# Cross attention and Fourier mixing on one core: the first batch's tables, layer 1 and stores put in another order

## The chip, the cores and the metric

The kernel runs on one core of a Trainium2 chip. TensorE (PE, with its weight loads PEld), VectorE (DVE), ScalarE (ACT), GpSimd (POOL) and SyncE (SP) each work through their own list of instructions in order and wait for each other on semaphores. The metric is the time on the device in microseconds (us), lower is better.

## The reference

Two blocks follow each other. The first is attention in both directions between 512 positions and 32 states, in 8 batches of 8 heads with 64 columns:

```python
scores = scale * np.matmul(x, state.transpose(0, 1, 3, 2))
a = softmax(scores);   xread = np.matmul(a, state)
scores2 = scale * np.matmul(state, x.transpose(0, 1, 3, 2))
a2 = softmax(scores2); sread = np.matmul(a2, x)
return np.concatenate([xread, sread], axis=2)        # 8 x 8 x 544 x 64
```

The second takes the 544 rows of 512 columns of each batch through a two-dimensional Fourier transform, a normalisation and two layers:

```python
mixed = np.real(np.fft.fft(np.fft.fft(x, axis=1), axis=2))
u = x + mixed
un = (u - mu) / np.sqrt(var + 1e-06)
return u + np.maximum(un @ w_ch1, 0.0) @ w_ch2        # 512 -> 2048 -> 512
```

## The kernel before

Each batch goes through three parts. `attend(b)` turns the states and x on PE (`turn_state`, `turn_x`: tiles sTp and xTp, copied to sT and xT), forms the exponentials twice (ET by state, E by position), reads with them (`xread`, `sread`: tiles xrp, xfp, xlp, srp, which become the rows XR, XF, XL) and folds the rows (XE, XO, XN). `transform(b)` multiplies the folded rows with cosine and sine tables over the 544 rows (`over_s`, tiles gp, copied to G) and then with tables over the 512 columns (`over_d`, T2, tiles yp), adds the rows (U), takes mean and variance, centres (ub) and turns the result (tiles tp, copied to unT). A batch has four tiles of 128 rows: row block k in 0 and 1, as it stands or mirrored (r = 1); the 32 rows left over in the middle, the low rows, are gathered over four batches. `layer1` and `layer2` are the two layers (tiles ph, which ACT brings to hT, and po, which VectorE scales by the row's deviation and adds to U in `store`).

The tables are made on the chip before the first batch needs them: a counter times a row number is brought into one period ("turned") on VectorE, `turn` for the 544 rows and `second_turn` for the 512 columns; ACT takes sines of both (`sines`, `more_sines`), and two of the four column tables are quarter turns of the other two, eight strided multiplications on POOL.

The order of every engine is written out by hand: `weave` takes streams of steps, each with a begin and an end between 0 and 1, and issues all steps by their place. `warm(n)` adds n matmuls on the identity matrix whose result nobody reads; `warmed` puts them behind each step of a stream. Loads of x go out on SP's queue (for batch 0 partly on ACT's); one small load puts row 0 into a partition that a large load has just filled, so it waits for that load. The weights are loaded by POOL, behind small copies into `gate` that hold POOL back. A mirrored tile is first written to `r_dram` and copied from there to the output in reversed row order; the low rows go through `l_dram` in the same way. In the last batch the mirrored tiles are stored on ACT's queue. Buffers for ot are 4, psum tiles with tag c 3, with tag q 3, and one pair of banks for x.

Of the kernel before, what the change touches and what calls it, by code (L numbers as in the profile page):

```python
# [12 lines left out]
F32 = mybir.dt.float32  # L13
BF16 = mybir.dt.bfloat16
I32 = mybir.dt.int32
AF = mybir.ActivationFunctionType
# [12 lines left out]
def kernel(  # L29
# [67 lines left out]
    def load_x(b):  # L97
        xs = wk.tile([128, 4, dm], F32, name="xs", tag="xs")
        xb = x[b].rearrange("h s d -> s h d")
        for n, (ps, si, rows) in enumerate((  # L100
            (slice(0, 128), 2, xb[256:384]),
            (slice(0, 128), 0, xb[1:129]),
            (slice(0, 1), 2, xb[0:1]),
            (slice(0, 128), 1, xb[129:257]),
            (slice(0, 128), 3, xb[384:512]),
        )):
            queue = nc.scalar if b == 0 and n in (1, 4) else nc.sync
            queue.dma_start(out=xs[ps, si, :].rearrange("p (h d) -> p h d", d=D), in_=rows)
        xs_of[b] = xs

    def cast_x(b):
        xs, t = xs_of[b], xin_bufs[b % 2]
        if b == 0:
            for si in (0, 2, 1, 3):
# [84 lines left out]

    def second_turn():  # L200
        nc.vector.tensor_copy(l2, li)
# [21 lines left out]
    def more_sines():  # L223
        w = 2.0 * PI / dm * shrink
        nc.scalar.activation(T2[:, 0, :], q2_, AF.Sin, bias=halfpi, scale=-w)
        nc.scalar.activation(T2[:, 2, :], f2, AF.Sin, bias=0.0, scale=-w)
        nc.scalar.activation(gate2[:, 3:4], gate2[:, 0:1], AF.Exp)
        c4 = [T2[:, i, :].rearrange("p (n r) -> p r n", r=4) for i in range(4)]
        for r in range(4):
            near, far = (0, 2) if r % 2 == 0 else (2, 0)  # L230
            for o, i, sign in ((1, near, 1.0 if r < 2 else -1.0), (3, far, 1.0 if r in (0, 3) else -1.0)):
                nc.gpsimd.tensor_scalar(c4[o][:, r, :], in0=c4[i][:, r, :], scalar1=sign, scalar2=None, op0=ALU.mult)
# [37 lines left out]
    def more_states():  # L270
        nc.vector.memset(stb[:, 2:].rearrange("p b g c -> p (b g c)").bitcast(F32), 0.0)
        state_ones(2, B)

# [17 lines left out]
    def attend(b):  # L291
# [19 lines left out]
        def turn_x(g):  # L311
            p = qt("xTp", BF16)
            for si in (0, 2, 1, 3):
                for k in range(2):
# [107 lines left out]
    def transform(b):  # L422
# [72 lines left out]
        if b == 0:  # L495
# [3 lines left out]
                lambda: (add(0, 0), centre(0, 0), turn_u(0, 1)),  # L499
                lambda: turn_u(0, 0),  # L500
                lambda: (add(1, 1), centre(1, 1)),
                lambda: (add(1, 0), centre(1, 0), turn_u(1, 1)),
                lambda: (turn_u(1, 0), done())]
# [45 lines left out]
    def layer1(key):  # L549
# [15 lines left out]

        def half_step(i, r):
            ph = psF.tile([128, 512], F32, name="ph", tag="c")
            cols = slice(256 * r, 256 * r + 256)
            for f in (2 * i, 2 * i + 1):
                for c in range(DC):  # L570
                    nc.tensor.matmul(ph[:, 256 * (f % 2):256 * (f % 2) + 256], lhsT=w1[:, c, f * 128:(f + 1) * 128],  # L571
                                     rhs=un_of[key][:, c, cols], start=(c == 0), stop=(c == DC - 1))
            nc.scalar.activation(hT[:, 2 * i:2 * i + 2, cols], ph.rearrange("p (a b) -> p a b", b=256), AF.Relu,
                                 scale=-1.0 if key in flipped else 1.0)

        if key == 0:
            return [lambda i=i, r=r: half_step(i, r) for r in range(2) for i in range(FC // 2)]
        return [lambda i=i: step(i) for i in range(FC // per)]

    def layer2(key):  # L580
# [4 lines left out]
        def store(i, cols):  # L585
# [7 lines left out]
            elif isinstance(dst, int):  # L593
                nc.sync.dma_start(out=l_dram[dst].rearrange("b r n -> (b r) n"), in_=ot)
                rows = out[4 * dst:4 * dst + 4]
                nc.sync.dma_start(out=rows[:, 257:288, :].rearrange("b r n -> r b n"),
                                  in_=l_dram[dst][:, 1:NL, :].rearrange("b r n -> r b n"))
                nc.sync.dma_start(out=rows[:, 0:1, :], in_=l_dram[dst][:, 0:1, :])
            else:
# [3 lines left out]
                queue.dma_start(  # L603
                    out=out[b, top:top - 128:-1, :].rearrange("r (c n) -> c r n", c=8),
                    in_=r_dram[b, k].rearrange("r (c n) -> c r n", c=8))

# [37 lines left out]
    def warmed(steps, n):  # L644
        return [lambda s=s: (s(), warm(n)) for s in steps if s is not None]
# [10 lines left out]
    weave((warmed(t0[4:8], 2), 0, 1), (s1[3:4], 0, 0))  # L656
# [53 lines left out]
```

## Time and profile before

| | us |
|---|---|
| median of 3 runs | 364.56 (364.07 to 364.62) |
| the profiled execution's own time | 364.14 |
| its span in the profile | 362.4 |
| PE busy | 325.5 (90%) |
| DVE busy | 175.8 (49%) |
| ACT busy | 158.6 (44%) |
| POOL busy | 65.6 (18%) |

A row of the timeline gives start, duration, engine, line, operation, output<-input, shapes, count, and in brackets the idle time before it with what ended it. Engine names with a q (SPq, ACTq) are queues that issue transfers: the duration there is that of the issue, not of the transfer. Matmul rows that follow each other overlap by about 0.2 us, since a result leaves the array after the next has begun. A row by stretch gives its length, the busy time of each engine with the number of instructions, the granted clock of TensorE as a share of full speed, the mean busy share of the 16 DMA engines and GB/s.

### The profile page before, as it was taken

What the parts mean: (1) busy time and instruction counts of PE and PEld (TensorE: products, weight loads), DVE (VectorE), ACT (ScalarE), POOL (GpSimd) and SP (SyncE); (2) the same over time, 40 slices, a digit from 0 to 9 for tenths busy, and PEclk for the clock granted to TensorE, in tenths of its full rate; (3) what the DMA queues carried; (4) which work ended last, traced back from release to release, by engine and by line L of the source; (5) the groups of instructions that cost most, each with busy time, mean ns of one, the idle gap of its engine ahead of it and who ended that gap; (6) DMA issues with size and microseconds to landing.
All of it is one profiled execution on the core that took longest, in us unless ns stands there. A gap on an engine that the chain in (4) does not pass through costs nothing.

```text
span 362.4 us, 5627 instructions
## 1 busy us (share of the span) xinstructions
PE 325.5 (90%) x2198; PEld 189.8 (52%) x2232; DVE 175.8 (49%) x432; ACT 158.6 (44%) x299; POOL 65.6 (18%) x150
## 2 busy tenths in 40 slices
PE   6747688899999999998999999999999999979970
PEld 6725566655555555555555555545554544445450
DVE  7697465645475537661454628462847173000120
ACT  4852664943464346333464345534553342433100
POOL 4099820500050003200140004000300030000000
PEclk9967899999999999999999999999999999999996
DMA  6889997005211511043101122020202020211123
GB/s 126 166 131 167 182 193 145 2 29 131 60 45 56 127 52 56 31 123 113 29 31 37 52 58 60 29 59 29 58 31 59 31 58 37 81 38 51 61 78 93
DMA packets 61556, 27.11 MB, mean 75 GB/s; under 512 B 52698, under 2 KB 57050, under 8 KB 61530
## 3 DMA queue, kind: packets, MB, share of 16 engines
q1 hardware_dynamic: 52874, 20.99, 22.4%
q0 software_dynamic: 4224, 4.19, 7.1%
q10 hardware_dynamic: 4432, 1.57, 1.8%
q8 instruction: 17, 0.28, 0.3%
q14 instruction: 9, 0.07, 0.1%
HBM read 22.04 MB, written 13.63 MB: 98 GB/s over the span
## 4 chain that ended last, share of the span: by engine, by line
PE 78%; DVE 11%; ACT 4%; DMA 2%; issue 2%; SPq 0%; DVEq 0%; ACTq 0%
PE po L622 30%; PE ph L561 27%; PE gp L439 3%; PE yp L457 3%; PE ph L571 2%; DMA xs<-in_x_dram 2%; PE xTp L316 2%; PE eTp L325 2%; PE srp L372 2%; PE tp L481 2%; DVE st L282 1%; ACT ub L474 1%; PE po L614 1%; PE xfp L353 1%; PE xrp L353 1%
## 5 line engine op out<-in xcount | busy, mean ns | idle before, releaser
L622 PE MATMUL po<-w,hT 128*128 128x512 bf16 x482 | 122.6, 379 | 1.6 <-ACT hT L563 0.9
L563 ACT ACTIVATE hT<-ph 128x512 bf16<-128x512 f32 x112 | 66.8, 597 | 121.2 <-PE ph L561 117.2
L561 PE MATMUL ph<-unT,w 128*128 128x512 bf16 x434 | 113.7, 379 | 2.9 <-ACT hTL L563 1.4
L561 PEld LDWEIGHTS <-w 128*128 128x128 bf16 x576 | 51.3, 98 | 55.6 <-issue 4.8
L622 PEld LDWEIGHTS <-hT 128*128 128x128 bf16 x496 | 47.7, 98 | 45.1 <-issue 1.3
L588 DVE SCALAR_TENSOR_TENSOR ot<-po,rstd,U 128x512 f32<-128x512 f32 (+1 forms) x33 | 24.2, 733 | 46.4 <-PE po L622 41.3
L449 POOL COPY GL<-G 128x128 bf16<-128x128 bf16 x8 | 2.4, 300 | 151.6 <-ACT G L447 151.6
L463 DVE TENSOR_TENSOR U<-yp,XR 128x511 f32<-128x511 f32 x16 | 10.9, 683 | 25.7 <-PE yp L457 24.6
L282 DVE BATCH_NORM_STATS2 st<-U 128x6 f32<-128x512 f32 x32 | 21.8, 680 | 0.1
L287 POOL TENSOR_TENSOR rstd<-rstd,mhalf 128x1 f32<-128x1 f32 x34 | 20.1, 591 | 2.7
L447 ACT CAST G<-gp 128x288 bf16<-128x288 f32 x30 | 11.9, 398 | 19.1 <-PE gp L439 13.1
L286 POOL TENSOR_TENSOR rstd<-mv,epst 128x1 f32<-128x1 f32 x34 | 6.6, 193 | 67.8 <-DVE mv L284 67.8
L483 ACT COPY unT<-tp 128x512 bf16<-128x512 bf16 x32 | 18.4, 588 | 0.4 <-PE tp L481 0.2
L317 DVE COPY xT<-xTp 128x1024 bf16<-128x1024 bf16 x10 | 6.9, 691 | 22.6 <-PE xTp L316 22.5
L571 PE MATMUL ph<-unT,w 128*128 128x256 bf16 x128 | 17.3, 282 | 0.5 <-ACT unT L483 0.5
L642 PE MATMUL warm<-ident 128*128 128x128 bf16 x144 | 14.2, 249 | 3.7 <-POOL halfpi L80 3.4
L457 PE MATMUL yp<-T,G 128*128 128x512 bf16 x60 | 16.1, 379 | 0.2
L481 PE MATMUL tp<-ident,ub 128*128 128x128 bf16 x128 | 11.8, 219 | 4.7 <-ACT ub L474 3.8
L383 ACT ACTIVATE XR<-srp,rcs 32x64 bf16<-32x64 f32 x32 | 9.9, 310 | 12.6 <-DVE rcs L374 12.3
L642 PEld LDWEIGHTS <-ident 128*128 128x128 bf16 x144 | 11.8, 114 | 6.3 <-POOL halfpi L80 3.4
L481 PEld LDWEIGHTS <-ub 128*128 128x128 bf16 x128 | 9.0, 98 | 10.3 <-ACT ub L474 4.5
L571 PEld LDWEIGHTS <-w 128*128 128x128 bf16 x128 | 12.6, 101 | 2.5 <-issue 0.7
(139 smaller groups left out, 391.0 us busy)
## 6 DMA issues: line engine op xcount, KB each, us to landing
xs<-in_x_dram SPq DMA_DIRECT2D x30, 256.0 KB
w<-in_moe_w_ch_dram POOLq DMA_DIRECT2D x8, 512.0 KB, 9.1
out_dram<-ot SPq DMA_DIRECT2D x15, 256.0 KB
r_dram<-ot SPq DMA_DIRECT2D x14, 256.0 KB
out_dram<-r_dram SPq DMA_DIRECT2D x14, 256.0 KB
xs<-in_x_dram ACTq DMA_DIRECT2D x2, 256.0 KB
l_dram<-ot SPq DMA_DIRECT2D x2, 256.0 KB
r_dram<-ot ACTq DMA_DIRECT2D x2, 256.0 KB
```

The lines of the kernel that those rows point to most:

```text
L282: nc.vector.bn_stats(st6, u)
L287: nc.gpsimd.tensor_tensor(rstd, rstd, mhalf, op=ALU.pow)
L447: nc.scalar.copy(G[:, j, :], p[:, 0:NM])
L457: nc.tensor.matmul(yp, lhsT=G[:, c, 128 * k:128 * k + 128], rhs=T2[:, c, :], start=(c == 0), stop=(c == 3))
L481: nc.tensor.transpose(tp[:, 128 * j:128 * j + 128], ub[k, r][:, 128 * j:128 * j + 128], ident)
L483: nc.scalar.copy(unT[:, :, col:col + 128], tp[:, 0:512].rearrange("p (a b) -> p a b", b=128))
L561: nc.tensor.matmul(ph[:, o:o + n], lhsT=w1[:, c, f * 128:(f + 1) * 128], rhs=un_of[key][:, c, :], start=(c == 0), stop=(c == DC - 1))
L563: nc.scalar.activation(hT[:, per * i:per * i + per, :].rearrange("p a b -> p (a b)"), ph, AF.Relu, scale=-1.0 if key in flipped else 1.0)
L571: nc.tensor.matmul(ph[:, 256 * (f % 2):256 * (f % 2) + 256], lhsT=w1[:, c, f * 128:(f + 1) * 128], rhs=un_of[key][:, c, cols], start=(c == ...
L588: nc.vector.scalar_tensor_tensor(ot[:, cols], in0=po_of[i][:, 0:cols.stop - cols.start], scalar=rstd, in1=u[:, cols], op0=ALU.mult, op1=AL ...
L622: nc.tensor.matmul(po_of[i], lhsT=h_of[key][:, f, i * 128:(i + 1) * 128], rhs=w2[:, f, :], start=(f == 0), stop=(f == FC - 1))
L642: nc.tensor.matmul(t[:, 0:128], lhsT=ident, rhs=ident, start=(i == 0), stop=(i == n - 1))
```

## The change

Eight edits, the first six in the front, up to the end of batch 0:

- The one-row load of x goes last of the five in each batch, no longer between the large ones; the casts and turns of x follow that order.
- The second turn runs right behind the first one, ahead of sT's and xT's copies. POOL's first gate waits for its end.
- Of the eight quarter turns four go to ACT.
- `warmed` bursts behind the last three score steps go; 48 warming matmuls come at the end of batch 0's reads. POOL's cast of batch 1's x moves ahead of the low rows' tables.
- The clearing of the state blocks of batches 2 to 7 moves from VectorE to POOL, the ones in it (eight small memsets on VectorE) into layer 1's stretch.
- Layer 1 of batch 0 goes tile by tile: 16 steps of four 128-column products for one tile of rows, instead of 16 steps of two 256-column products for two tiles.
- The places of the streams beside layer 1 of batch 0 shift, and layer 1 of batch 1 begins at 0.08 of its stage instead of 0.02.
- Mirrored tiles are copied in 16 column pieces of 32 (before: 8 of 64), low rows in 16 column pieces by batch (before: whole rows, outermost the row number).

VectorE's order at the start. gen is the scratch of the two turns (128x864 the first, 128x512 the second); before:

```order
L175 SCALAR_TENSOR_TENSOR gen_78<-gen_78 128x864
L309 COPY sT<-sTp 128x512
L317 COPY xT<-xTp 128x1024 x2
L201 CAST gen_79<-gen_79 128x512
L202 TENSOR_SCALAR gen_79<-gen_79,pf 128x512
L203 TENSOR_SCALAR gen_79<-gen_79 128x512
L204 TENSOR_SCALAR gen_79<-gen_79 128x512
L205 TENSOR_TENSOR gen_79<-gen_79 128x512
L175 SCALAR_TENSOR_TENSOR gen_79<-gen_79 128x512
L133 CAST stb<-stf 32x2x64 x4
L361 RECIPROCAL rs<-xrp 128x8
```

And now, on the same engine at the same place:

```order
L175 SCALAR_TENSOR_TENSOR gen_78<-gen_78 128x864
L201 CAST gen_79<-gen_79 128x512
L202 TENSOR_SCALAR gen_79<-gen_79,pf 128x512
L203 TENSOR_SCALAR gen_79<-gen_79 128x512
L204 TENSOR_SCALAR gen_79<-gen_79 128x512
L205 TENSOR_TENSOR gen_79<-gen_79 128x512
L175 SCALAR_TENSOR_TENSOR gen_79<-gen_79 128x512
L308 COPY sT<-sTp 128x512
L316 COPY xT<-xTp 128x1024 x2
L133 CAST stb<-stf 32x2x64 x4
L360 RECIPROCAL rs<-xrp 128x8
```

The six rows of the second turn moved from between xT and the first reciprocal to ahead of sT.

ACT's order where layer 1 of batch 0 begins (ub is the centred tile, unT its turned copy, hT layer 1's result, ET and E belong to batch 1); before:

```order
L474 ACTIVATE ub<-U,mv 128x512 x2
L483 COPY unT<-tp 128x4x128 x2
L573 ACTIVATE hT<-ph 128x2x256
L327 ACTIVATE ET<-eTp 128x512
L474 ACTIVATE ub<-U,mv 128x512 x2
L483 COPY unT<-tp 128x4x128
L573 ACTIVATE hT<-ph 128x2x256
L341 ACTIVATE E<-esp 128x512
```

Now:

```order
L473 ACTIVATE ub<-U,mv 128x512 x2
L482 COPY unT<-tp 128x4x128
L572 ACTIVATE hT<-ph 128x4x128
L482 COPY unT<-tp 128x4x128
L572 ACTIVATE hT<-ph 128x4x128
L473 ACTIVATE ub<-U,mv 128x512
L326 ACTIVATE ET<-eTp 128x512
L572 ACTIVATE hT<-ph 128x4x128
```

The first result of layer 1 now comes behind one copy of unT, and two more come before batch 1's second ET and the third ub.

SP's order at the end of the program, from the last batch's low rows on; before:

```order
L594 DMA l_dram<-ot 128x512
L596 DMA out_dram<-l_dram 31x4x512
L598 DMA out_dram<-l_dram 4x512
L592 DMA out_dram<-ot 128x512
L592 DMA out_dram<-ot 128x256 x2
```

Now:

```order
L593 DMA l_dram<-ot 128x512
L595 DMA out_dram<-l_dram 16x31x32 x4
L597 DMA out_dram<-l_dram 16x4x32
L591 DMA out_dram<-ot 128x512
L591 DMA out_dram<-ot 128x256 x2
```

One copy of 31 rows by four batches became four copies with 16 as the outermost count. On ACT's queue the two mirrored tiles of the last batch change from 8x128x64 to 16x128x32 at unchanged places.

The diff, cut:

```diff
-            (slice(0, 1), 2, xb[0:1]),
             (slice(0, 128), 1, xb[129:257]),
             (slice(0, 128), 3, xb[384:512]),
+            (slice(0, 1), 2, xb[0:1]),
...
-    def second_turn():
+    def turn2():
...
-        state_blocks(1, 2, nc.vector.tensor_copy)
+
+    turn2()
...
-            for o, i, sign in ((1, near, 1.0 if r < 2 else -1.0), (3, far, 1.0 if r in (0, 3) else -1.0)):
-                nc.gpsimd.tensor_scalar(c4[o][:, r, :], in0=c4[i][:, r, :], scalar1=sign, scalar2=None, op0=ALU.mult)
+            nc.scalar.activation(c4[1][:, r, :], c4[near][:, r, :], AF.Copy, scale=1.0 if r < 2 else -1.0)
+            nc.gpsimd.tensor_scalar(c4[3][:, r, :], in0=c4[far][:, r, :], scalar1=1.0 if r in (0, 3) else -1.0,
+                                    scalar2=None, op0=ALU.mult)
...
-    nc.gpsimd.tensor_copy(gate, q1[:, 2, 0:4])
+    nc.gpsimd.tensor_copy(gate, q2_[:, 0:4])
...
+        nc.gpsimd.memset(stb[:, 2:].rearrange("p b g c -> p (b g c)").bitcast(F32), 0.0)
...
-        def half_step(i, r):
+        def quarter_step(i, r):
             ph = psF.tile([128, 512], F32, name="ph", tag="c")
+            for f in range(4 * i, 4 * i + 4):
+                o = 128 * (f % 4)
                 for c in range(DC):
+                    nc.tensor.matmul(ph[:, o:o + 128], lhsT=w1[:, c, f * 128:(f + 1) * 128],
+                                     rhs=un_of[key][:, c, 128 * r:128 * r + 128], start=(c == 0), stop=(c == DC - 1))
...
+                for bq in range(4):
+                    nc.sync.dma_start(out=out[4 * dst + bq, 257:288, :].rearrange("r (c n) -> c r n", c=16),
+                                      in_=l_dram[dst, bq, 1:NL, :].rearrange("r (c n) -> c r n", c=16))
...
-                    out=out[b, top:top - 128:-1, :].rearrange("r (c n) -> c r n", c=8),
-                    in_=r_dram[b, k].rearrange("r (c n) -> c r n", c=8))
+                    out=out[b, top:top - 128:-1, :].rearrange("r (c n) -> c r n", c=16),
+                    in_=r_dram[b, k].rearrange("r (c n) -> c r n", c=16))
...
-    weave((warmed(s0, 8), 0, 1), ([second_turn], 0.6, 0.6))
-    weave((warmed(r0, 4), 0, 1), ([sines], 0.01, 0.01), ([more_sines], 0.3, 0.3), ([lambda: cast_x(1)], 0.25, 0.25))
-    more_states()
+    weave((warmed(s0[:4], 8) + s0[4:], 0, 1), ([lambda: state_blocks(1, 2, nc.vector.tensor_copy)], 0.6, 0.6))
+    weave((warmed(r0, 4), 0, 1), ([sines], 0.01, 0.01), ([more_sines], 0.3, 0.3), ([lambda: cast_x(1)], 0.0, 0.0),
+          ([lambda: warm(48)], 1, 1))
...
-    weave((layer1(0), 0, 1), (t0[8:], 0.03, 0.15), (s1[4:], 0.0, 0.2), (reads_next, 0.22, 0.5),
-          (transform(1), 0.52, 1.0), ([lambda: cast_x(2)], 0, 0), (scores_next, 0.55, 0.95),
-          ([lambda: load_x(4)], 0.8, 0.8))
+    weave((layer1(0), 0, 1), (t0[7:], 0.02, 0.3), (s1[4:], 0.12, 0.3), (reads_next, 0.28, 0.54),
+          (transform(1), 0.6, 1.0), ([lambda: cast_x(2)], 0.1, 0.1), (scores_next, 0.5, 0.95),
+          ([lambda: state_ones(2, B)], 0.5, 0.5), ([lambda: load_x(4)], 0.8, 0.8))
...
-            streams.append((layer1(b), 0.02, 1))
+            streams.append((layer1(b), 0.08 if b == 1 else 0.02, 1))
```

More of the change, by code (lines that the diff above doesn't have):

```diff
@@ L102, in load_x @@
             (slice(0, 128), 0, xb[1:129]),
-            (slice(0, 1), 2, xb[0:1]),
             (slice(0, 128), 1, xb[129:257]),
             (slice(0, 128), 3, xb[384:512]),
+            (slice(0, 1), 2, xb[0:1]),
         )):
-            queue = nc.scalar if b == 0 and n in (1, 4) else nc.sync
+            queue = nc.scalar if b == 0 and n in (1, 3) else nc.sync
             queue.dma_start(out=xs[ps, si, :].rearrange("p (h d) -> p h d", d=D), in_=rows)
@@ L113, in cast_x @@
         if b == 0:
-            for si in (0, 2, 1, 3):
+            for si in (0, 1, 3, 2):
                 nc.scalar.copy(t[:, si, 1:513], xs[:, si, :])
@@ L268, in more_loads @@
             nc.gpsimd.dma_start(out=w2[:, q * 4:(q + 1) * 4, :], in_=w2v[:, q * 4:(q + 1) * 4, :])
-    def more_states():
-        nc.vector.memset(stb[:, 2:].rearrange("p b g c -> p (b g c)").bitcast(F32), 0.0)
-        state_ones(2, B)
     def qt(name, dt=F32):
@@ L312, in turn_x @@
             p = qt("xTp", BF16)
-            for si in (0, 2, 1, 3):
+            for si in (0, 1, 3, 2):
                 for k in range(2):
@@ L499, in transform @@
                 lambda: (add(0, 0), centre(0, 0), turn_u(0, 1)),
-                lambda: turn_u(0, 0),
-                lambda: (add(1, 1), centre(1, 1)),
-                lambda: (add(1, 0), centre(1, 0), turn_u(1, 1)),
+                lambda: (turn_u(0, 0), add(1, 1)),
+                lambda: (centre(1, 1), add(1, 0)),
+                lambda: (centre(1, 0), turn_u(1, 1)),
                 lambda: (turn_u(1, 0), done())]
@@ L564, in step @@
                                  scale=-1.0 if key in flipped else 1.0)
-        def half_step(i, r):
+        def quarter_step(i, r):
             ph = psF.tile([128, 512], F32, name="ph", tag="c")
-            cols = slice(256 * r, 256 * r + 256)
-            for f in (2 * i, 2 * i + 1):
+            for f in range(4 * i, 4 * i + 4):
+                o = 128 * (f % 4)
                 for c in range(DC):
[L571 to L574, printed above, removed]
+                    nc.tensor.matmul(ph[:, o:o + 128], lhsT=w1[:, c, f * 128:(f + 1) * 128],
+                                     rhs=un_of[key][:, c, 128 * r:128 * r + 128], start=(c == 0), stop=(c == DC - 1))
+            nc.scalar.activation(hT[:, 4 * i:4 * i + 4, 128 * r:128 * r + 128], ph.rearrange("p (a b) -> p a b", b=128),
+                                 AF.Relu, scale=-1.0 if key in flipped else 1.0)
         if key == 0:
-            return [lambda i=i, r=r: half_step(i, r) for r in range(2) for i in range(FC // 2)]
+            return [lambda i=i, r=r: quarter_step(i, r) for r in range(4) for i in range(FC // 4)]
         return [lambda i=i: step(i) for i in range(FC // per)]
@@ L594, in store @@
                 nc.sync.dma_start(out=l_dram[dst].rearrange("b r n -> (b r) n"), in_=ot)
[L595 to L598, printed above, removed]
+                for bq in range(4):
+                    nc.sync.dma_start(out=out[4 * dst + bq, 257:288, :].rearrange("r (c n) -> c r n", c=16),
+                                      in_=l_dram[dst, bq, 1:NL, :].rearrange("r (c n) -> c r n", c=16))
+                nc.sync.dma_start(out=out[4 * dst:4 * dst + 4, 0, :].rearrange("b (c n) -> c b n", c=16),
+                                  in_=l_dram[dst, :, 0, :].rearrange("b (c n) -> c b n", c=16))
             else:
```

2 lines of the change are left out of this document (1 added, 1 removed).

## The prediction

> **What bounds the kernel now.** I read the page's slices first, then busy time by stage, then the chain at both ends. The page:
>
> ```profile
> span 362.4 us, 5627 instructions
> ...
> PE   6747688899999999998999999999999999979970
> ...
> PEclk9967899999999999999999999999999999999996
> ```
>
> TensorE is filled in the middle; the holes are in the first seven slices and in the last. The stages, cut where the program changes (start:end, length, then busy us of PE, PEld, DVE, ACT, POOL, granted clock, DMA share, GB/s):
>
> ```profile
> 17.00:26.47 9.47, 3.74 (x33) 2.57 (x31) 8.80 (x26) 6.33 (x13) 7.70 (x11) 0.72 0.74 118
> 26.47:38.97 12.50, 8.94 (x66) 6.39 (x68) 9.76 (x28) 3.90 (x7) 10.96 (x27) 0.77 0.93 171
> 38.97:47.00 8.03, 6.73 (x65) 5.28 (x65) 1.20 (x4) 5.60 (x11) 7.39 (x13) 0.84 1.06 183
> 47.00:56.50 9.50, 6.57 (x56) 4.91 (x53) 7.52 (x22) 4.45 (x10) 0.88 (x3) 1.00 1.21 208
> 70.53:80.00 9.47, 8.48 (x46) 4.39 (x45) 3.94 (x11) 5.11 (x12) 0.65 (x1) 1.00 0.00 0
> 80.00:340.00 260.00, 254.11 (x1571) 137.11 (x1600) 122.24 (x283) 112.06 (x212) 29.82 (x62) 1.00 0.20 59
> 351.50:362.40 10.90, 0.00 (x0) 0.00 (x0) 0.44 (x1) 0.00 (x0) 0.00 (x0) 0.69 0.33 96
> ```
>
> From 80 to 340 PE works 254.1 of 260 us, and from the last tile of batch 0's layer 2 on PE's order is the same in both kernels: that stretch only shifts. What can change is the front (VectorE bounds 17 to 26.5, PE at a reduced clock 26.5 to 39) and the 10.9 us in which nothing but stores is left.
>
> **The end.** Rows of SP's and ACT's queues (start, us in issue, line), one row of VectorE, and two windows:
>
> ```profile
> 324.03 0.68 SPq L603 DMA_DIRECT2D out_dram<-r_dram  x1
> 338.43 0.32 SPq L594 DMA_DIRECT2D l_dram<-ot  x1
> 340.45 0.64 SPq L596 DMA_DIRECT2D out_dram<-l_dram  x1
> 341.84 0.35 ACTq L602 DMA_DIRECT2D r_dram<-ot  x1
> 348.13 1.26 ACTq L603 DMA_DIRECT2D out_dram<-r_dram  x1
> 349.49 3.62 ACTq L602 DMA_DIRECT2D r_dram<-ot  x1
> 356.92 0.68 ACTq L603 DMA_DIRECT2D out_dram<-r_dram  x1
> 351.45 0.48 DVE L588 SCALAR_TENSOR_TENSOR ot<-po,rstd,U 128x256 f32<-128x256 f32 x1 [1.26 <-PE po L614]
> 324.00:328.00 4.00, 3.58 (x29) 2.16 (x29) 0.00 (x0) 0.97 (x2) 0.00 (x0) 1.00 0.29 66
> 344.00:348.00 4.00, 4.00 (x22) 1.88 (x20) 0.75 (x1) 0.00 (x0) 0.00 (x0) 1.00 0.06 25
> ```
>
> The staging write of the low rows lands 2.02 us after its issue (338.43 to 340.45, where the copy that waits for it goes out). Then 31x4x512 runs: the share is 0.06, one engine of 16, at 25 GB/s; its 254 KB take 10.2 us by that rate, to about 351. The mirrored tile's staging write, issued at 341.84, lands only at 348.13 (6.3 us instead of 2.0), the next one 7.4 us after its issue, and the span ends 5.5 us after the last mirrored copy went out (356.92). By contrast the copy at 324.03, with an outermost count of 8, ran undisturbed: 0.29 x 4 us x 16 = 18.6 engine-us for 1024 pieces of 256 B, 18 ns each, 128 pieces on each of 8 engines = 2.3 us, landed some 4 us after its issue.
>
> With an outermost count of 16 the pieces should spread over all engines. Low rows: 4 x 496 pieces, 124 on each engine; mirrored tile: 2048 pieces, again 128 on each. A 128-byte piece is in no row; between half the price of a 256-byte one (9 ns) and twice it (36), I take the same 18 ns, since the rows at 344 (2 KB pieces, 82 ns at 25 GB/s) against 18 ns for 256 B point to a large fixed part. SP issues five copies instead of two, 3 x 0.64 = 1.9 us more, done by about 344 and hidden: its next store is the tile that comes out near 349. Then: first staging write lands at 343.9; its copy 4.1 later, at 348.0; the second staging write shares the first copy's completion counter in the new order and so waits for it, lands 350.4; its copy ends the span 5.5 us after issue, 355.9. The last plain store (VectorE ends at 351.9, plus issue 0.3 and 2.0) is not later. Gain 362.4 - 355.9 = **6.5 us**. At 36 ns each copy takes 2.3 more, twice in a row: gain 1.9; at 9 ns the plain store and its closing limit it: gain about 7.
>
> The Trainium skill ("DMA: Bandwidth & Descriptors", Specifications) gives 512 B as the least transfer for line rate and read-modify-write below: it speaks against smaller pieces. The 256-byte pieces here already lie below; by its rule the halved piece moves half the bytes at the same cost or worse, which is 6.5 us at equal cost and 1.9 at the doubled one.
>
> **The front.** Rows in the order of the argument (bracket: idle before, and what ended it):
>
> ```profile
> 3.41 4.77 PE L642 MATMUL warm<-ident 128*128 128x128 bf16 x48 [3.41 <-POOL halfpi L80]
> 6.63 1.06 DVE L175 SCALAR_TENSOR_TENSOR gen<-gen 128x864 f32<-128x864 f32 x1
> 11.33 0.69 DVE L317 COPY xT<-xTp 128x1024 bf16<-128x1024 bf16 x1 [2.46 <-PE xTp L316]
> 12.84 0.42 DVE L201 CAST gen<-gen 128x512 f32<-128x512 int32 x1
> 15.46 0.69 DVE L175 SCALAR_TENSOR_TENSOR gen<-gen 128x512 f32<-128x512 f32 x1
> 14.67 1.28 ACT L341 ACTIVATE E<-esp 128x512 bf16<-128x512 f32 x2
> 17.00 0.21 DVE L361 RECIPROCAL rs<-xrp 128x8 f32<-128x8 f32 x1
> 17.93 0.16 DVE L374 RECIPROCAL rcs<-srp 128x1 f32<-128x1 f32 x1
> 21.49 1.23 DVE L387 TENSOR_TENSOR XE<-XL 32x256 bf16<-32x256 bf16 x1
> L387 DVE TENSOR_TENSOR XE<-XL x8: 281/284/1233, 21.5 to 273.9; 32x256 bf16<-32x256 bf16 x8
> 24.00:28.00 4.00, 1.52 (x11) 1.25 (x12) 3.56 (x8) 0.40 (x1) 4.00 (x6) 0.50 1.25 207
> 28.00:31.40 3.40, 2.87 (x21) 2.18 (x19) 2.89 (x13) 0.00 (x0) 3.40 (x13) 0.50 1.22 198
> 26.47 0.37 PEld L439 LDWEIGHTS <-XE 128*128 128x128 bf16 x3 [3.85 <-DVE XE L393]
> 24.89 5.14 POOL L232 TENSOR_SCALAR T<-T 128x128 bf16<-128x128 bf16 x8
> 27.20 1.38 DVE L271 MEMSET stb<- 128x1584 f32 x1 [0.27 <-issue]
> 29.43 0.42 DVE L309 COPY sT<-sTp 128x512 bf16<-128x512 bf16 x1
> 32.80 0.81 PE L457 MATMUL yp<-T,G 128*128 128x512 bf16 x3
> 38.97 1.87 PE L571 MATMUL ph<-unT,w 128*128 128x256 bf16 x8 [0.49 <-ACT unT L483]
> ```
>
> *Loads and second turn.* The second turn takes 12.84 to 16.15 = 3.3 us of VectorE, in front of the first reciprocal at 17.00. Moved behind the first turn (ends 7.69) it ends near 11.0, and sT's copy (0.42) brings xT to 11.4: where it is now. So the x tiles, which arrive earlier when SP no longer stands at the one-row load, gain nothing: VectorE is their cover. The gain comes behind: VectorE is free, and what ends last is ACT's pair of E (14.67 to 15.95). Three bursts of eight warming matmuls leave PE's path to it, so about 0.65 earlier; srp follows, and rcs moves from 17.93 to 15.9. Between 1.3 (E not earlier) and 2.4; I take **2.0**.
>
> *XE of the low rows* takes 1.23 us once where the median is 0.284: 0.95 of stall while POOL issues w1's loads. Those go out earlier (they wait for x of batch 1, whose loads are no longer interrupted), but batch 1's cast on POOL now follows them directly and may stand there instead. **0.5** (-1.0 to 0.95). The Trainium skill ("SBUF — State Buffer", Who interferes with whom) has a two-input VectorE operation wait for a whole GpSimd instruction that reads SBUF. By it the cast takes back what the issue gave: the front's sum would be 0.5 lower. By the trace, Sm, XE and XO beside POOL's quarter turns ran at their usual times, and the 0.5 stays.
>
> *Tables and first products.* The memset and eight small ones hold VectorE from 27.20 to 29.43; on POOL the memset is off the path (a like amount is saved there: four of eight quarter turns, 2.6 us; the weights of layer 2, loaded behind it, are first used near 70). ACT's four quarter turns of 128x128 cost at most the 0.64 each of an E of 128x512, 2.6 in all, behind its sines (T2 ends near 21.3) and before G's first cast; they need no other table, since ACT already scales the state reads with the same function between sines. But from 26.47 to 32.80 PE itself was the bound, at half clock until 31.4, and stood only about 0.5 us for VectorE. The 48 added matmuls (the first 48 took 4.77 us, at the 66 ns each of the 128-column row below they need 3.2) start when the last xrp is in, near 20, and end at 23.2 to 24.8 against XE at 24.0. If they hold the clock, the 6.3 us shrink to some 3.5, all wait lists counted at full rate; if not, by 0.5 and less 0.8 of delay. **1.6** (-0.3 to 2.8).
>
> *First layer-1 step.* It now waits for one turned tile, not two: one 128x512 operation on ACT sooner (0.64 by the E rows). **0.6** (0 to 0.9).
>
> *Layer 1 tile by tile.*
>
> ```profile
> 57.48 1.04 PE L571 MATMUL ph<-unT,w 128*128 128x256 bf16 x8
> 327.01 1.06 PE L561 MATMUL ph<-unTL,w 128*128 128x128 bf16 x16
> ```
>
> Sixteen matmuls of 128 columns take 1.06 us, eight of 256 take 1.04; sixteen steps: 0.3 more, weight loads included. Five steps instead of four now stand ahead of batch 1's reads, and sTp and the first xTp move into the read chain, where PE idles 2.9 of 9.5 us: 0.87 + 0.6 less at its end. Against it the 0.3 and the eight small memsets, 0.85 together (28.58 to 29.43), part of them beside a wait in that chain. **0.6** (0 to 1.5).
>
> *Layer 1 of batch 1* begins at 0.08 instead of 0.02 of its stage. PE idles 1.0 us of 9.47 there, against 2.3% later. **0.5** (0 to 0.8).
>
> Front 2.0 + 0.5 + 1.6 + 0.6 + 0.6 + 0.5 = 5.8, end 6.5, together 12.3. Against the profiled execution's 364.14: 351.8; the median of the runs shown is 364.56, 0.4 above it, within what a measurement can tell (0.2%, 0.7 us). I forecast **351.8**.
>
> **The rivals.**
>
> *Half of the front is lost* (20%): the clock stays low and the warming matmuls push the first product, so that only 2 us of the front and 0.8 of batch 1 remain: 364.1 - 2.8 - 6.5 = 354.8. For it: the granted clock of 0.72 and 0.77. Against: the rows' VectorE work is gone either way. The skill's "TensorE: Matmul & The Clock Gate" (Part 1) drops the clock after an idle window of 3.4 us and restores it after a busy one; no row shows the window with these 48 in it.
>
> *The small pieces cost double* (14%): 364.1 - 5.8 - 1.9 = 356.4. Against: the fixed part seen above.
>
> *More than forecast* (6%): clock held and every term near its bound: front 8.5, end 7: 348.6.
>
> *Slower* (3%): the mirrored copies, two in a row at the end, take so long that they eat everything. The end is 343.9 + copy + 2.4 + copy + 1.4, less the front's 5.8; it passes 362.4 only where a copy takes over 10 us, 128 pieces at above 65 ns. The one-engine copy moved whole 2 KB pieces at 82, so only if a piece's price did not depend on its size at all.
>
> *The change doesn't do what it says* (2%): the column cut doesn't spread over the engines and the front is bound elsewhere: 364.
>
> **How the numbers follow.** The likeliest case (55%) has its own range of 349.5 to 353.5, from front terms of 4.5 to 7.5 and an end of 6 to 7. With half-lost fronts and double-priced pieces the range is 348.8 to 356.6, leaving a little below and some 8% above. Faster by over 0.2%: 95%; within: 2%; slower: 3%.
>
> **What would show it.** Right: no window of share 0.06 after the last low rows; the staging writes of ACT land 2 us after issue; PE's end to span's end 4 to 5 us instead of 10.9; first rcs near 16, first product with T by 28, first layer-1 step by 33, first po near 64.5. Wrong: share above 0.5 for over 4 us after a mirrored copy; half clock from 21 to 28 as before; ACT's queue the releaser of layer 1's steps.

## The result and the profile after

The kernel after takes 351.77 us (median of 4 runs, 351.69 to 352.26), the kernel before 364.59 on the same chip: a ratio of 0.9654 (95% interval 0.9637 to 0.9671). The forecast was 351.8. But that number came out by misses that cancel. The times at which VectorE writes the output tiles (`store`) tell where the 12.5 us between the two spans lie:

| start of a store on VectorE, us | before | after | lead |
|---|---|---|---|
| second of batch 2, ahead of layer 1 of the low rows of batches 0 to 3 | 161.50 | 161.07 | 0.43 |
| last of batch 2, behind it | 183.33 | 180.81 | 2.52 |
| second of batch 6, ahead of layer 1 of the low rows of batches 4 to 7 | 313.39 | 310.87 | 2.52 |
| last of batch 6, behind it | 330.75 | 325.69 | 5.06 |
| last of all | 351.45 | 346.40 | 5.05 |

So the front gave 0.43 us (forecast: 5.8), two stages in the middle (those of batches 3 and 7, which hold the low rows) gave 4.62 where the forecast had a stretch that "only shifts", and the end, from PE's last matmul to the end of the span, shrank from 10.94 to 3.55 us, 7.4 (forecast: 6.5). Without the 4.6 us in the middle the kernel would stand at some 356.4, outside the 349.5 to 353.5 of the forecast's likeliest case: that the number was met is luck.

The page of the kernel after, slices of TensorE and its granted clock:

```profile
span 349.9 us, 5931 instructions
...
PE   6857688899999999999999999999999999999995
...
PEclk9998899999999999999999999999999999999999
```

The empty slice at the end is gone; the holes of the front are still there. The end, SP's and ACT's queues, the last store, and three windows (busy us of PE, PEld, DVE, ACT, POOL, clock, DMA share, GB/s; the first is behind the mirrored copy issued at 320.70 and little else):

```profile
335.38 2.59 SPq L595 DMA_DIRECT2D out_dram<-l_dram  x4
336.78 0.37 ACTq L602 DMA_DIRECT2D r_dram<-ot  x1
339.06 0.67 ACTq L603 DMA_DIRECT2D out_dram<-r_dram  x1
342.60 0.35 ACTq L602 DMA_DIRECT2D r_dram<-ot  x1
344.65 0.56 ACTq L603 DMA_DIRECT2D out_dram<-r_dram  x1
343.68 3.56 SPq L591 DMA_DIRECT2D out_dram<-ot  x3
346.40 0.48 DVE L587 SCALAR_TENSOR_TENSOR ot<-po,rstd,U 128x256 f32<-128x256 f32 x1 [1.26 <-PE po L614]
320.70:324.70 4.00, 4.00 (x32) 2.32 (x31) 0.00 (x0) 1.79 (x3) 0.00 (x0) 1.00 0.43 70
340.00:344.00 4.00, 4.00 (x26) 2.35 (x24) 0.95 (x2) 0.00 (x0) 0.00 (x0) 1.00 0.55 117
344.00:348.00 4.00, 2.36 (x22) 1.86 (x20) 0.97 (x2) 0.00 (x0) 0.00 (x0) 1.00 0.77 196
```

No window of share 0.06 is left. ACT's first staging write lands after 2.28 us (336.78 to 339.06) instead of 6.3, the second after 2.05 instead of 7.4. The second copy goes out at 344.65, still ahead of the last plain store, which now ends the span. A copy of 2048 pieces of 128 bytes costs at most 0.43 x 4 x 16 = 27.5 us of one DMA engine, 13.4 ns a piece; the forecast took 18.

The front, in the order of the argument (VectorE's rows of the fold, POOL beside them, PE behind them). An operation that is held up while it runs shows as a longer row; the text says that it stood:

```profile
19.06 1.22 DVE L386 TENSOR_TENSOR XE<-XL 32x256 bf16<-32x256 bf16 x1
20.21 1.97 DVE L387 TENSOR_TENSOR XO<-XL 32x255 bf16<-32x255 bf16 x1
24.29 0.70 DVE L391 TENSOR_TENSOR Sm<-XF,XR 128x1028 bf16<-128x1028 bf16 x1
25.70 2.77 DVE L394 COPY XN<-Sm 128x2 bf16<-128x2 bf16 x1
25.77 2.71 DVE L308 COPY sT<-sTp 128x512 bf16<-128x512 bf16 x1
16.88 3.19 POOL L259 DMA_DIRECT2D w<-in_moe_w_ch_dram  x4 [0.35 <-issue]
20.02 2.02 POOL L117 CAST xin<-xs 128x2048 bf16<-128x2048 f32 x1
24.46 1.09 POOL L233 TENSOR_SCALAR T<-T 128x128 bf16<-128x128 bf16 x1
25.36 0.48 POOL L236 MEMSET T<- 1x256 bf16 x1
27.03 1.41 POOL L263 MEMSET stb<- 128x1584 f32 x1
25.50 0.42 PE L438 MATMUL gp<-CT,XE 128*128 128x288 bf16 x2 [2.76 <-DVE XE L392]
28.55 0.64 PE L438 MATMUL gp<-CT,XE 128*128 128x288 bf16 x2 [1.95 <-DVE xT L316]
38.13 1.86 PE L570 MATMUL ph<-unT,w 128*128 128x128 bf16 x16 [1.48 <-ACT unT L482]
28.00:32.00 4.00, 3.45 (x24) 2.72 (x24) 1.62 (x5) 0.27 (x1) 3.75 (x9) 0.58 1.22 218
```

XE ends 0.2 us behind POOL's issue of w1's loads (20.07), XO 0.1 behind POOL's cast (22.04), XN when POOL's row of clears ends (28.44). XN has two columns, and sT's copy, behind it in VectorE's order, waits with it. PE stands for 2.76 and 1.95 us, and from 28 on its clock is at 0.58.

The middle, groups of PE (busy us, mean ns, then idle us ahead of them and what ended it), first of the kernel before, then of the kernel after:

```profile
L622 PE MATMUL po<-w,hT 128*128 128x512 bf16 x482 | 122.6, 379 | 1.6 <-ACT hT L563 0.9
L561 PE MATMUL ph<-unT,w 128*128 128x512 bf16 x434 | 113.7, 379 | 2.9 <-ACT hTL L563 1.4 <-ACT unT L483 0.9
L561 PE MATMUL ph<-unTL,w 128*128 128x128 bf16 x128 | 8.4, 219 | 1.4 <-ACT hT L563 1.4
```

```profile
L622 PE MATMUL po<-w,hT 128*128 128x512 bf16 x478 | 122.1, 379 | 0.8
L560 PE MATMUL ph<-unT,w 128*128 128x512 bf16 x437 | 113.9, 379 | 0.6
L560 PE MATMUL ph<-unTL,w 128*128 128x128 bf16 x128 | 8.5, 219 | 0.0
```

PE's order is the same in both, and yet layer 1 of the low rows waited for ACT's hT before and doesn't now. The edits don't touch these lines. What differs in the built programs is the bank of the tiles with tag c in PSUM, the memory that PE writes its results to; the pool chooses it when the program is built. In the stage of batch 3, where low rows and rows of a batch alternate (phL is a low-row step):

```
before  ph 5  phL 6  ph 5  po 6  ph 5  phL 5  ph 5  phL 5  ph 5  po 5
after   ph 7  phL 5  ph 7  po 5  ph 6  phL 7  ph 6  phL 7  ph 6  po 5
```

Before, six tiles in a row share a bank, so that PE can begin each of the last five only when the one just ahead of it has been emptied by ACT. The next section tries whether that is the cause.

### The profile page after: what moved, and what is told of

It reads as the page before. It is cut to its first block, busy times and chain, and to the rows that moved or that the text cites. A ratio compares the mean times of both kernels' runs of the same rounds, so it can differ in the third digit from the quotient of the medians.

```text
span 349.9 us, 5931 instructions
## 1 busy us (share of the span) xinstructions
PE 326.0 (93%) x2347; PEld 193.1 (55%) x2382; DVE 177.0 (51%) x431; ACT 159.3 (46%) x303; POOL 64.4 (18%) x147
## 3 DMA queue, kind: packets, MB, share of 16 engines
HBM read 22.04 MB, written 13.63 MB: 102 GB/s over the span
## 4 chain that ended last, share of the span: by engine, by line
PE 81%; DVE 12%; ACT 3%; issue 1%; POOL 0%; DVEq 0%; POOLq 0%; ACTq 0%
PE po L622 31%; PE ph L560 29%; PE gp L438 3%; PE yp L456 3%; PE ph L570 2%; PE eTp L324 2%; PE srp L371 2%; PE tp L480 2%; PE xTp L315 2%; ACT ub L473 1%; DVE st L281 1%; PE po L614 1%; PE xrp L352 1%; PE gp L442 1%; PE xfp L352 1%
## 5 line engine op out<-in xcount | busy, mean ns | idle before, releaser
L560 PEld LDWEIGHTS <-w 128*128 128x128 bf16 x576 | 51.1, 98 | 50.1
L570 PE MATMUL ph<-unT,w 128*128 128x128 bf16 x256 | 18.2, 229 | 1.5 <-ACT unT L482 1.5
L570 PEld LDWEIGHTS <-w 128*128 128x128 bf16 x256 | 16.7, 103 | 2.1 <-issue 1.6
L316 DVE COPY xT<-xTp 128x1024 bf16<-128x1024 bf16 x10 | 7.9, 803 | 16.7 <-PE xTp L315 16.7
L642 PEld LDWEIGHTS <-ident 128*128 128x128 bf16 x166 | 12.6, 110 | 5.5 <-POOL halfpi L80 3.4
```

Of the source, the lines that this page charges most:

```text
L560: nc.tensor.matmul(ph[:, o:o + n], lhsT=w1[:, c, f * 128:(f + 1) * 128], rhs=un_of[key][:, c, :], start=(c == 0), stop=(c == DC - 1))
L570: nc.tensor.matmul(ph[:, o:o + 128], lhsT=w1[:, c, f * 128:(f + 1) * 128], rhs=un_of[key][:, c, 128 * r:128 * r + 128], start=(c == 0), st ...
L642: nc.tensor.matmul(t[:, 0:128], lhsT=ident, rhs=ident, start=(i == 0), stop=(i == n - 1))
```

## The experiments

In these kernels (but for after_again) each tile's PSUM bank is written out by a table, so that an edit in one place can't change the choice in another.

**The middle: the banks alone.** banks_in_before is the kernel before with the banks of the kernel after from the stage of batch 3 on, banks_in_after the reverse. The edit, in short:

```diff
-ph = psF.tile([128, 512], F32, name="ph", tag="c")
+ph = psF.tile([128, 512], F32, name="ph", tag="c" + BANKS[n], bufs=1)   # n: number of the tile
```

> The kernel before, unchanged but for the PSUM bank of each tile with tag c from the stage of batch 3 on: the sequence of the kernel after, where no tile takes the bank of the tile just ahead of it. Theory: the 4.6 us that the stages of batches 3 and 7 lost come from this alone: 360.0 us, the waits of layer 1 behind ACT's hT (0.69, 0.69, 0.24 us near 165, 172 and 173) gone. Rival 1 (these waits come from another place, such as the phase of ACT's work or of the store copies): 364.6, no change. Rival 2 (only the stage of batch 3, since that of batch 7 was helped by the stores): about 362.5.

360.38 us (ratio 0.9857, 0.9817 to 0.9897), 4.6 less than the 365.01 of the kernel before beside it. The store rows gain 2.09 us in the stage of batch 3 and 2.54 in that of batch 7, nothing elsewhere, and the waits are gone:

```profile
L642 PE MATMUL po<-w,hT 128*128 128x512 bf16 x496 | 124.8, 379 | 0.0
L581 PE MATMUL ph<-unTL,w 128*128 128x128 bf16 x128 | 8.5, 219 | 0.0
```

> The kernel after, unchanged but for the PSUM banks of the tiles with tag c from the stage of batch 3 on: the sequence of the kernel before, in which six tiles in a row share one bank. Theory: the 4.6 us come back: 356.4 us. Rival 1 (the banks don't matter): 351.8. Rival 2 (a part of it is hidden in the end, since the low rows' stores then have longer): about 355.

Three of its runs took 355.8 to 356.4 us, as the theory has it; no trace of them was kept. The fourth, the profiled one, took 350.0, though its two stages lose just as much (its lead over the kernel before stays at 6.59 us through both, and the waits are back: 1.4 us ahead of the low-row steps). It is its front that is 6.2 us shorter than in the kernel after, with the same instructions:

```profile
18.02 3.19 POOL L278 DMA_DIRECT2D w<-in_moe_w_ch_dram  x4 [0.35 <-issue]
21.16 1.95 POOL L136 CAST xin<-xs 128x2048 bf16<-128x2048 f32 x1
19.06 0.28 DVE L406 TENSOR_TENSOR XE<-XL 32x256 bf16<-32x256 bf16 x1
21.65 2.02 DVE L411 TENSOR_TENSOR Sm<-XF,XR 128x1028 bf16<-128x1028 bf16 x1
24.29 0.42 PE L458 MATMUL gp<-CT,XE 128*128 128x288 bf16 x2 [1.55 <-DVE XE L412]
33.60 1.05 PE L590 MATMUL ph<-unT,w 128*128 128x128 bf16 x16 [1.48 <-ACT unT L502]
65.05 1.03 PE L642 MATMUL po<-w,hT 128*128 128x512 bf16 x4
```

Here batch 1's x landed 1.1 us later, POOL issued w1's loads at 18.02 instead of 16.88, and XE and XO slipped through at 0.28 beside the second of its four loads. Only Sm met the cast. The first gp came 1.2 us earlier, XN met no clear, the clock stayed at 1.00, and the first po stood at 65.05 instead of 71.20. A chance has shown what the front is worth. It also speaks for pricing a front by several profiles.

**The front: POOL's clears.** late_clear moves the big clear and the state's copies far back on POOL, clears_later moves all clears by 2.5 us:

```diff
 def more_loads():
-    clears(1)
-    nc.gpsimd.memset(stb[:, 2:]..., 0.0)
     for hh in range(1, 4):
         low_tables(hh)
+    clears(1)
+    nc.gpsimd.memset(stb[:, 2:]..., 0.0)     # late_clear: this and state_blocks behind cast_x(2), clears(1) stays
```

> The kernel after with the clearing of the state blocks of batches 2 to 7 (1.41 us) and their copies (3.43 us) moved on POOL from 27 us to behind the cast of batch 2's x, near 43; all PSUM banks as in the kernel after. Theory 1 (VectorE's copy of XN, 2.77 us instead of 0.27, waits for POOL's clearing, and sT's and xT's copies behind it): XN takes under 0.5 us, the second tile gp starts 1.5 to 2 us earlier than 28.55, PE has no gap of 2 us there, and the first yp comes 1.5 to 2.5 us earlier: 349.8 us. Theory 2 (XN waits for the row of seven small clears at 25.4 to 27.0): XN ends at about 27.0 and the gain is 1.0 us at most: 350.9. Rival (the front is held by something else, such as weights that arrive later): rows at 26 change and the first po stays at 71.2: 351.8.

> The kernel after with POOL's seven small clears and the clearing of the state blocks moved by 2.5 us on POOL alone, behind the three pairs of low table copies. Theory (VectorE's copy of XN, 128x2 from bf16 to bf16, waits for any clear that runs on POOL): XN takes 0.3 us if the clears begin after 26.0, and as in late_clear or longer if not; the small clears of T remain at 25.4 to 26.1, so XN ends near 26.2, the second gp starts near 26.7 instead of 28.55, and the first yp 1.5 to 2 us earlier: 350.0 us. Rival (copies of tables on POOL stall it as well): XN ends at 28.4 as now, 351.8.

350.91 and 350.61 us. XN in the first, with the last small clear beside it, then in the second, with the clear of T's row:

```profile
25.95 1.41 DVE L416 COPY XN<-Sm 128x2 bf16<-128x2 bf16 x1
26.92 0.41 POOL L268 MEMSET XN<- 128x384 bf16 x1
```

```profile
25.98 0.46 DVE L414 COPY XN<-Sm 128x2 bf16<-128x2 bf16 x1
26.04 0.38 POOL L256 MEMSET T<- 1x256 bf16 x1
```

It ends with the row of clears each time (27.36 and 27.33, 26.44 and 26.42): theory 2 of the first was right, and the clears of T's row hold it as the others do. Against the kernel after the stores come 0.93 and 1.52 us earlier. The rival of the second fell by its numbers (28.4, 351.8), but no table copy ran beside XN there. In w1_early_clears below one did, and XN took 0.39 us and ended 0.03 behind it (25.25 and 25.22): a table copy can hold it too, though not for a whole row of copies.

**The front: POOL's issue and cast.**

```diff
-nc.gpsimd.tensor_copy(gate, xs_of[1][:, :, 0])        # w1's loads no longer wait for batch 1's x
-    ([lambda: cast_x(1)], 0.0, 0.0)
+    ([lambda: cast_x(1)], 0.25, 0.25)                  # w1_early_clears; in w1_early_gaps_filled 0.0
-weave((warmed(t0[4:7], 2), 0, 1), ...)
+weave((warmed(t0[4:5], 2) + warmed(t0[5:7], 20), 0, 1), ...)      # w1_early_gaps_filled alone
```

> As clears_later, and POOL issues the loads of w1 right behind its first clears, near 12 us, instead of waiting for batch 1's x near 16.3; the cast of batch 1's x goes back behind the first pair of low table copies. Theory (what held the front in the kernel after is VectorE standing for POOL: XE 1.22 and XO 1.97 us instead of 0.28 each while POOL issued w1's loads and cast x, then XN): XE and XO take 0.28, the fold ends 2.5 us earlier, the first gp starts near 23 right behind the warming matmuls, PE has no gap of 2 us, the clock stays at 1.00 and the first po comes 5 us earlier or more: 346 us. Rival 1 (the cast of x moves onto Sm instead): first gp at 24.3, still without a drop of the clock: 347.5. Rival 2 (batch 1's x comes late, since w1's loads take its bandwidth): the transposes of batch 1 wait, 351 or slower.

347.48 us (ratio 0.9501, 0.945 to 0.9552). Rival 1 by its numbers: the first gp starts at 24.44, but the cast now meets XE (1.85 us, until 0.1 behind the cast), not Sm. The clock holds until the gaps of 1.46 and 1.48 us ahead of layer 1, where the first ph takes 1.71 us. The profiled run of banks_in_after has the same two gaps at full clock. The records of the clock tell why: it changes only on a grid of 3.41 us (last section), and here both gaps fall into one step of it, there into two (first row w1_early_clears, then banks_in_after; the first number behind the length is PE's busy time, and the clock falls to half at 34.08):

```profile
30.66:34.08 3.42, 0.72 (x10) 0.60 (x11) 3.25 (x9) 1.92 (x3) 2.94 (x6) 1.00 0.00 0
28.73:32.15 3.42, 1.93 (x16) 1.04 (x15) 2.91 (x7) 0.82 (x2) 3.27 (x7) 1.00 1.21 200
32.15:35.56 3.41, 1.96 (x36) 1.96 (x36) 3.13 (x8) 2.01 (x4) 3.20 (x5) 1.00 1.14 235
```

So the next kernel moves the cast and fills the gaps:

> As w1_early_clears, but the cast of batch 1's x stands ahead of the low table copies again (it now runs as soon as that x is in), and the two gaps of PE behind the products with T (30.3 to 31.9 and 32.3 to 33.9 us) are filled with 20 warming matmuls each instead of 2. Theory (VectorE stands wherever a POOL instruction on SBUF runs beside its SBUF operations, and PE's clock drops after gaps): XE takes 0.28 us instead of 1.85, the first gp starts 1.5 us earlier, near 22.9, the first ph takes 1.06 us instead of 1.71 and the first two together 1.4 us less: 345.0 us. Rival 1 (x lands only near 18.5, so that the cast stalls XE as before): the gain is the clock's alone, 346.2. Rival 2 (the added warming matmuls hold up the transposes of the centred tiles): slower than 347.5.

345.77 us (345.57 to 347.24; ratio 0.9493, 0.9461 to 0.9525), beside 352.11 of after_again on the same chip:

```profile
12.11 3.19 POOL L277 DMA_DIRECT2D w<-in_moe_w_ch_dram  x4
17.30 1.89 POOL L136 CAST xin<-xs 128x2048 bf16<-128x2048 f32 x1 [2.00 <-DMA xs<-in_x_dram]
19.06 0.28 DVE L405 TENSOR_TENSOR XE<-XL 32x256 bf16<-32x256 bf16 x1
23.29 0.27 DVE L413 COPY XN<-Sm 128x2 bf16<-128x2 bf16 x1
23.10 0.42 PE L457 MATMUL gp<-CT,XE 128*128 128x288 bf16 x2 [0.36 <-DVE XE L411]
32.30 1.05 PE L589 MATMUL ph<-unT,w 128*128 128x128 bf16 x16 [0.47 <-ACT unT L501]
63.76 1.03 PE L641 MATMUL po<-w,hT 128*128 128x512 bf16 x3
```

Hardly an operation stands for POOL any more, the clock is at 1.00 in each window from 16 to 44, and the first po comes 7.44 us earlier than in the kernel after. The two edits were not run apart, so their prices are known only from these rows. 1.3 of the 7.44 are lost at the end, where this run's last stores took 4.9 us behind PE instead of 3.55: the last batch's second staging write goes out 4.95 us behind the first mirrored copy (331.62 to 336.57) instead of 3.54 (339.06 to 342.60), and the second copy, issued only when PE has ended, now ends the span. Why the first copy landed later stays open. The kernel beats both others.

> The kernel after, unchanged, beside the next two on one chip. By its first runs: 351.8 us, PE's clock 0.99. If the front's length hangs on when batch 1's x lands and so on where POOL's issue of w1's loads meets VectorE's work, a run of about 346 at clock 1.00 can occur.

352.11 us (351.23 to 352.83), x again early (POOL's issue at 17.25): no run at full clock among these.

**The 48 warming matmuls.** no_warm_48:

```diff
-          ([lambda: warm(48)], 1, 1))
```

> The kernel after without the 48 warming matmuls at the end of batch 0's reads. Theory 1 (they hold the clock at 1.00 until 28 us): without them the granted clock is 0.6 or lower from 20 to 28 us, the transposes of batch 1 and gp take up to twice as long from 25.5 on, and the time is 0.5 to 1.0 us longer: 352.5. Theory 2 (PE stands for VectorE there in any case, and the clock is back to half at 28 with them too): the same within 0.3, 351.8. Rival (they delay the state's turn): 0.3 faster.

352.18 us (351.79 to 353.06), beside 351.77 and 352.11 of the kernel after: theory 2. The clock does fall without them,

```profile
20.00:24.00 4.00, 0.00 (x0) 0.00 (x0) 3.90 (x9) 3.57 (x8) 4.00 (x6) 0.67 1.24 205
24.00:28.00 4.00, 1.97 (x13) 1.54 (x14) 3.86 (x7) 0.40 (x1) 4.00 (x13) 0.50 1.23 200
```

but in after_again it fell with them as well (0.69 from 24 to 28 us), since PE stood 3.13 us behind them. Alone they are worth at most a few tenths.

**Layer 1 tile by tile.** half_steps goes back to the half steps and before's streams in the kernel after, gaps_filled_half_steps in w1_early_gaps_filled:

```diff
-return [lambda i=i, r=r: quarter_step(i, r) for r in range(4) for i in range(FC // 4)]
+return [lambda i=i, r=r: half_step(i, r) for r in range(2) for i in range(FC // 2)]
```

> The kernel after with layer 1 of batch 0, its streams and the begin of layer 1 of batch 1 put back as before (16 half steps for two tiles); the PSUM banks of the later stages as in the kernel after. The forecast put 0.6 + 0.6 + 0.5 on these edits: by it this kernel takes 353.5 us. Theory now (in the kernel after the first layer 1 step came 0.84 us earlier than before, the first po 0.67 later, and the stores of batch 1 0.43 earlier, so the tile steps give nothing): 351.3 to 352.3. Rival (tile steps cost, since batch 1's reads wait behind more of them): 350.8, the first po at 70.3 or earlier.

350.93 us, but from 349.2 to 353.4, with mean clocks from 0.979 to 1.0: inconclusive. So it was tried again where the front has no stall:

> As w1_early_gaps_filled, but layer 1 of batch 0 in half steps, its streams and the begin of layer 1 of batch 1 as before (20, 12 and 6 warming matmuls in the gaps of PE there), so that the tile steps are priced in a front without stalls and at the full clock. The forecast gave the tile steps, their order and the later begin 1.7 us: by it 347.5. Theory from the traces (the half steps reach the first po 30.4 us behind the first step, the tile steps 31.5 at full clock, but the first step comes 0.6 to 1.5 later and the stage behind it has a wait of 0.94 more): within 0.7 of 345.8 us. Rival: the half steps are faster, 345.0.

345.49 us (345.22 to 346.48, 6 runs; ratio 0.9468, 0.9435 to 0.9501), the same as with tile steps. The edit of layer 1 is worth nothing measurable.

**The end.** stores_16 is the kernel before with the new stores alone, low_16 with those of the low rows alone:

```diff
+for bq in range(4):                        # low_16: this hunk alone
+    nc.sync.dma_start(out=out[4 * dst + bq, 257:288, :].rearrange("r (c n) -> c r n", c=16), ...)
-in_=r_dram[b, k].rearrange("r (c n) -> c r n", c=8))
+in_=r_dram[b, k].rearrange("r (c n) -> c r n", c=16))
```

> The kernel before with only the stores of the change (mirrored tiles and low rows in 16 column pieces), and every PSUM tile held in the bank that it has in the kernel before. Theory: the end alone is worth what the two traces show there, the time from PE's end to the span's end falling from 10.9 to about 3.5 us: 357.2 us, and PE's last row still ends at 351.4. Rival 1 (the stores also disturb or help the middle): the store rows of VectorE in the stages of batches 3 and 7 move by more than 0.3 us. Rival 2 (the end is worth the 6.5 of the forecast and the rest came from PE finishing at another time against the low rows): 358.1.

> The kernel before with only the low rows stored in 16 column pieces, the mirrored tiles in 8 as before, PSUM banks as before. Theory: the low rows' one-engine copy was what held the end, since the mirrored tile's staging write waited behind it (6.3 us instead of 2.0); nearly all of the end's gain is here: 358 to 359 us against 364.6, and the span ends 4 to 5 us behind PE. Rival (the mirrored tiles' 8 pieces cost as much): the gain is only half, about 361.

357.8 us (ratio 0.9802, 0.977 to 0.9833) and 358.42 (0.9831, 0.9784 to 0.9878). In stores_16 PE ends at 352.10 and the span at 355.4, 3.3 us behind it, and no store of the middle moves against the others: the end is worth 7.6 us in this trace. In low_16 PE's end and the span's are still 4.6 us apart (350.43 to 355.0), so the low rows' copy was 6.4 of it, as the theory has it, and the mirrored tiles' pieces 1.2.

## Why the forecast held, and where it failed

*The end, 6.5:* right in its mechanism; 7.4 came. The step that was mis-sized is the chain of the mirrored tiles: the piece costs at most 13.4 ns, not 18, so that both copies land sooner and the plain store limits the end, which the forecast had named as the bound of about 7. The Trainium skill ("DMA: Bandwidth & Descriptors", Specifications) keeps line rate for transfers of 512 B or more: 128 bytes cost three quarters of 256 here (13.4 and 18 ns), so by bytes 1.5 times as much, which agrees in direction. The rival built on a doubled piece (356.4) is out, since the piece became cheaper.

*"That stretch only shifts":* false. Same order of PE was taken for same time; the banks were not looked at. The two stages gave 4.62 us, and banks_in_before gives all of it (4.63) without any other edit. The first sign stood in the trace of before, in the group of layer 1 that waits for hT 1.4 us, and the forecast read PE's 98% as full.

*The front, 5.8:* failed. By the lead over the kernel before at each step:

| term | forecast | measured by |
|---|---|---|
| second turn, state read | 2.0 | 2.44: rcs 17.93 to 15.49 |
| XE of the low rows | 0.5 | -1.47: first gp 26.47 to 25.50 |
| tables, first products, clock | 1.6 | -0.73: first yp 32.80 to 32.56 |
| first layer-1 step | 0.6 | 0.60: first ph 38.97 to 38.13 |
| tile by tile | 0.6 | -1.51: first po 70.53 to 71.20 |
| layer 1 of batch 1 later | 0.5 | 1.10: stores of batch 1, lead 0.43 |

The first held. The fourth held at its own row, as in the front without stalls (first ph 32.30 with tile steps, 32.94 with half steps), but nothing of it was left at the first po (63.76 and 63.36). The second failed at "the 0.5 stays": with w1's issue and the cast in one piece, XO stood 1.97 us where it had taken 0.50. The forecast had weighed the rule that a VectorE operation with two SBUF inputs contends with a POOL instruction that reads SBUF, in the Trainium skill ("SBUF — State Buffer", Who interferes with whom), and set it aside because Sm ran freely beside POOL's quarter turns. It did so again (0.70), but both times the turn that began beside it took longer (1.07 us before, 1.09 after, where a turn without such a neighbour takes 0.71): the two met there too, at POOL's cost, and the forecast had looked at VectorE's rows alone. Beside the cast it was VectorE that stood (XO, Sm 2.02, XE 1.85, each until the cast was done), as the rule has it. The forecast's reading of XE's 1.23 us in the kernel before was off as well: XE ended at 22.72, 0.57 behind POOL's issue and 0.14 behind the low table copy that followed it (22.58), so a part of that stall was the copy's.

The third failed at "on POOL the memset is off the path": a two-column copy, XN, waited for it, and the copies of sT and xT behind XN. By the same section of the Trainium skill a copy can contend with POOL for the ports that they share, and whoever comes second is blocked until the other's instruction is over; XN was blocked for a row of instructions, until the last clear. The gaps so made cost the clock, and the 1.6 with it: the first product with T came at 32.56 (announced: by 28), the first layer-1 step at 38.13 (33), the first po at 71.20 (64.5). The fifth term is nothing by gaps_filled_half_steps; the loss and the gain of the last two rows belong together (-0.41).

The rival "half of the front is lost" (354.8, 20%) was thus the true case for the front, and too mild. 351.8 was met only since 4.6 us turned up that nothing in the change aims at.

## What to carry to other kernels

An unchanged instruction order doesn't make an unchanged stretch: where a pool chooses buffers, compare which buffer each tile gets before calling a stage untouched, and look for tiles that follow each other in one. Before work goes to POOL to be out of the way, list what VectorE does beside it: here one small SBUF copy waited 2.5 us on a row of clears, longer than the moved ones had taken on VectorE (2.2 us, 27.20 to 29.43). A front with gaps of 1.5 to 3 us in PE has two prices, by how the gaps fall on the grid of the clock, and closing the gaps (POOL's work out of the fold's way, then warming matmuls in what is left) was worth 6.

## What the runs showed of the hardware

- A VectorE operation on two SBUF inputs (XE) stood until POOL's issue of four loads was over, 0.2 us behind its end in six profiles of the kernel after and its variants (XE 1.22 to 1.62 us instead of 0.28), where XE began in the third load's issue. In the profiled run of banks_in_after it began in the second one's and took 0.28: the issue doesn't hold it all the time, and which part of it does stays open.
- A copy from SBUF to SBUF waited for a whole row of back-to-back clears on POOL (2.77 us for 128x2), not only for the one that was running. Copies from PSUM were held only by standing behind it: in the kernel before, an xT copy ran beside the same clears in its usual 0.69 us (30.96, clears from 30.5 to 31.6).
- PE's granted clock changed only on a grid of 3.41 us: in all fourteen profiles every stretch at half clock (but the last, which the end cuts off) lasted 3.41, 6.83 or 10.24 us, and the grid lay differently against the kernel in each run (the clock's first record begins 6.10 to 9.31 us into the span). What separates the steps of the grid is PE's busy time in them, not the longest gap. At full clock, the 33 steps with 1.61 us or less were followed by half clock, and none of the 1337 with 1.65 us or more. At half clock, the 19 steps with 2.68 us or more were followed by full clock, and none of the 18 with 2.55 or less. In the kernel after the clock outlasted a step with 1.65 us of work (21.09 to 24.50) and fell behind the next, with 1.10 (24.50 to 27.91). The Trainium skill ("TensorE: Matmul & The Clock Gate", Part 1) has a free-running window of 3.4 us decide, and the traces agree; it drops the clock after an idle window, and here up to 1.61 us of work in the window did not prevent the drop.
